# Attention and MoE in one kernel: MoE rows split where they lie and turned by DMA, bounds spread by bfloat16 products, the shift row turned in float16, buffers shared anew, a new table of times

## The chip, the cores and the metric

The kernel runs on one core of a Trainium2 chip. The metric is the device time of one execution in microseconds; the median of three runs of the kernel before is 639.03 us (638.96 to 639.34). Smaller is better. PE is the matrix engine, DVE, ACT and POOL are the vector, scalar and GpSimd engines, SP is the queue from which nearly all DMAs are issued.

## What is computed

Queries of 1152 rows are averaged in pairs to 576; 4 batches of 8 heads of softmax attention with head size 64 follow, and their result, 2304 rows of 512, goes through a layer h = x w_in, e = softmax weights of h, solu = h e, a normalisation and a product with w_out.

```python
q_pool = q.reshape(B, H, S // factor, factor, D).mean(axis=3)
scores = scale * np.matmul(q_pool, k.transpose(0, 1, 3, 2))
attn = np.exp(scores - max) ; attn = attn / (sum + 1e-09) ; attn @ v
...
h = x @ w_in
sm = e / (np.sum(e, axis=-1, keepdims=True) + 1e-09)      # e = exp(h - max)
solu = h * sm
ln = (solu - mu) / np.sqrt(var + 1e-06) * g_ln
return ln @ w_out
```

## The kernel before, in words

All factors of a product are held as two float16 parts, a high one and what it leaves (`left`, `sub`), so that a float32 product is made of three or four float16 ones. The heads run in 16 pairs P (heads g = 2P and 2P+1); the first pair works in float32. Each head has nine key blocks j, and for each block PE makes the scores, ACT their exponential twice (`expo`, float16 and float32), POOL or DVE the difference of both (`rest`), and PE the products with the values. Ahead of that stand, for each head, the row maxima (`maxima`: products, DVE reductions, then `turn`, which turns the 4 or 5 columns of maxima into rows on PE, `shift`, which scales them into float16 `c5`, and `put`, a DMA that lays them under the queries as a further row of `q2`).

For each pair there are bounds: the largest |q| (`q_turn`), a sum of |v| (`v_turn`), and for each weight matrix the largest weight (`weight_scale`). Each is a column of 128 numbers, of which every partition needs the maximum: PE turns the column, widened to 128 x 128, with a float32 product against the identity (`ident`) and DVE reduces the result. There are 16 + 15 + 2 of them. `k_hi` and `k_lo` split the keys of a pair in SBUF; `k_lo` is two DVE instructions. Keys and queries are then turned by DMA transposes on the SP queue.

The MoE part (`tokens`) has 18 tiles n of 128 rows, four for each batch and one more for every second batch. A tile is: `turn`, four float32 PE products that turn x into PSUM (line 1291 of the profile); `x_hi` (ACT) and `x_lo` (DVE), which split it out of PSUM into `xh`, `xl`; 24 products with w_in; the softmax weights (`top`, `neg`, `expo`, `weigh`), statistics (`mean`, `total`, `inverse`, `square`, five small POOL steps `factor`) and `norm`; `turn2`, eight float32 products that turn the normed rows e into PSUM (line 1379), split there by `l_hi` (ACT) and `l_lo` (DVE); 24 products with w_out; a copy and two output DMAs of 64 rows. Tiles 13 to 17 belong to the last batch and run when no attention is left (`tail`); their tiles are named `et`, `xht`, `xlt`, `lht`, `llt`.

The order of everything is set by `Plan`: each step is added with an engine, a length, the steps it needs and a due time, to which the table `OFF` adds a number for each step; a list scheduler walks all engines in time and emits the instructions of each engine in the order found. SP's queue is one of these engines, so a DMA that waits holds those behind it. `tags` says which tiles share buffers and how many there are.

Of the kernel before, what the change touches and what calls it, by code (L numbers as in the profile page):

```python
# [10 lines left out]
F32 = mybir.dt.float32  # L11
# [11 lines left out]
KP = {'W': [2, 4.44, 37.52, 4.7], 'step': 1.05, 'M': [78.33, 15.88, 7.65], 'TX': 118, 'TP': 69, 'win': 4.28, 'P': [24.74, 18.81, 12.81, 18.34, 35, 22.83], 'QP': 29, 'N': [11.98, 7], 'AV': 5.18, 'CD': [[27, 53, 2], [69, 288, 10]], 'SD': [[12, 83, 5], [70, 287, 1]], 'VM': 'BCCCBCCCBCCBCCCB', 'OF': [4.76, 1.62, 9.84, 2.47, 1.86], 'N1': 8.51, 'warm': 1, 'ws': -3.83, 'GR': 0, 'GG': 13, 'b_eh': 6, 'b_w1': 4, 'V0': -98.83, 'VF': 1, 'QD': [0, 1], 'L0': 2.74, 'F': 0, 'EX': [[10, 71, 50], [42, 282, 0]], 'LX': [3, 36.19], 'HP': [146073, 0], 'DL': 2000, 'MA': 18.0, 'TR': [2000, 2], 'P1': [-3.89, -3.14, 3.71, -7.84, -10.1, 0.03], 'WS': [47, 70, 0.22], 'KD': 5.48, 'RB': [0, 1], 'RS': [2.5, 6.5], 'LO': 0.3}  # L23
# [19 lines left out]
class Plan:  # L43
# [20 lines left out]
    def __init__(self, tags, banks, window):  # L64
        self.tags, self.banks, self.window = tags, banks, window
        self.bank = {}
        self.warm, self.warm_until = None, 0
        self.ops = []
        self.parts, self.writers, self.readers = defaultdict(dict), {}, defaultdict(list)
        self.users = defaultdict(int)  # L70

    @staticmethod
    def group(k):

        i = k[2] if k[0] in ("w32", "wm", "wi", "wo") else k[1]
        return f"{k[0]}.{i[0] if isinstance(i, tuple) else i}"

    def _keys(self, keys):
        for k in keys:
            if len(k) == 2 and self.parts[k]:  # L80
                yield from list(self.parts[k])
            yield k

    def add(self, engine, length, at, fn, reads=(), writes=(), mark=None, kind="round", also=(), calls=1, port=0):
        at += OFF.get(self.group((writes or reads)[0]), 0)
        o = Op(n=len(self.ops), engine=engine, length=length, at=at, fn=fn, mark=mark, kind=kind, calls=calls)
        o.port = port or engine == "POOL"
        deps = o.deps
# [24 lines left out]
    def run(self):  # L113
# [85 lines left out]
        while events:  # L199
            t, what, _, arg = heapq.heappop(events)  # L200
            if what == 0:
                o, done = arg, done + 1
                for b in o.uses:
                    count[b] -= 1
                    for i in where[b]:
                        last[i][o.engine] = o
                    if not count[b]:
                        for i in where[b]:
                            held[i] = None
                        for e in ready:  # L210
                            push(t, 1, e)
                for m in after[o]:
                    e = m.engine
                    hop = self.HOP[o.engine][e] + (self.LOAD[m.kind] if e == "PE" != o.engine else 0)
                    if o.engine == e and not m.deps[o]:
                        hop = 0
                    elif e == "PE" != o.engine and t > PAD[0]:
                        hop += pad
                    m.ok_at = max(m.ok_at, t + hop)
                    m.left -= 1  # L220
                    if not m.left:
                        ready[e].append(m)
                        push(m.ok_at, 1, e)
                continue
            e = arg
            if busy[e] > t:
                continue
            best = None
            limit = 1e9 if not todo else now_mark + (self.window if todo < len(marks) else FIRST)
            for o in ready[e]:  # L230
                if o.at > limit or o.ok_at > t or (best is not None and (o.at, o.n) >= (best.at, best.n)):
                    continue
                g = buffers(o)
                if g is None:
                    continue
                s = could(o, g)
                if s > t:
                    push(s, 1, e)
                    continue
                best, got = o, g  # L240
            if best is None:
                if e == "PE" and self.warm and t > KP.get("ws", 2.5) * 1000 and todo > self.warm_until:
                    i = next((i for i in range(8) if held.get(i) is None), None)
                    if i is not None:
                        extra.append((t, lambda i=i: self.warm(i)))
                        busy[e] = t + (110 if t > self.COLD else 216)
# [81 lines left out]
def attention_solu_moe(  # L328
# [17 lines left out]
    NH = B * H  # L346
    NP = NH // 2
# [1225 lines left out]
```

## Time and profile before

| | us |
|---|---|
| median of 3 runs | 639.03 |
| the profiled execution | 640.0 |
| its span, first to last instruction | 638.2 |
| PE busy | 613.8 (96%) |
| DVE busy | 514.8 (81%) |
| ACT busy | 504.8 (79%) |
| POOL busy | 451.9 (71%) |

The profiled execution is 1.0 us over the median. The granted clock of PE is 1.0 but for the stretch from 20 to 40 us, where it is 0.91. Busy time of PE counts a product from its start to its modelled end, while products overlap; so a busy PE may still have short gaps, and what a product costs in a row is read from stretches of many.

### The profile page before, as it was taken

Reading aid. Unit: us, or ns where it says so; the run is one execution under the profiler, and the core shown is the slowest. Engines: PE = TensorE matmul, PEld = TensorE weight load, DVE = VectorE, ACT = ScalarE, POOL = GpSimd, SP = SyncE. Lnnn points to the kernel's source line nnn. Section 1 sums busy time; section 2 is a strip of 40 time slices with the busy share of each in tenths; the row PEclk is TensorE's granted clock in tenths of the full one; section 3 lists DMA queues with packets and bytes.
Section 4 is the critical chain, followed back from the end, with each engine's and each line's share of the span. In section 5 each row is a group of like instructions: output and inputs, shape, how many; then the busy total and the mean of one; then the engine's idle time right before and its main releaser. Section 6 shows DMA issues by size and latency. Waiting matters only on the chain.

```text
span 638.2 us, 17474 instructions
## 1 busy us (share of the span) xinstructions
PE 613.8 (96%) x6823; PEld 398.7 (62%) x6823; DVE 514.8 (81%) x1145; ACT 504.8 (79%) x966; POOL 451.9 (71%) x485
## 2 busy tenths in 40 slices
PE   8989899999989999999999999999999999999995
PEld 8866676676555665666656655666665666564552
DVE  8998898989999889888997888989899757455451
ACT  3777797999898988899888998888897988734442
POOL 3495564576679998989988997798988798720100
PEclk9899999999999999999999999999999999999999
DMA  8476869696928673665573655755681510001102
GB/s 226 133 178 144 191 172 190 181 196 117 182 29 178 102 150 75 116 126 114 120 121 86 118 126 110 133 111 97 104 175 37 86 35 13 18 9 34 33 1 49
DMA packets 161294, 70.49 MB, mean 110 GB/s; under 512 B 150332, under 2 KB 150332, under 8 KB 161212
## 3 DMA queue, kind: packets, MB, share of 16 engines
q1 hardware_dynamic: 161212, 69.38, 52.1%
q8 instruction: 53, 0.87, 0.6%
q14 instruction: 29, 0.24, 0.1%
HBM read 36.70 MB, written 4.72 MB: 65 GB/s over the span
## 4 chain that ended last, share of the span: by engine, by line
PE 75%; DVE 12%; ACT 5%; DMA 3%; POOL 2%; issue 2%; SPq 1%; ACTq 0%; POOLq 0%; DVEq 0%
PE bank L462 68%; DVE mx L959 3%; PE bank L1379 2%; PE bank L1541 2%; POOL eh L1115 1%; DVE kn L468 1%; PE bank L1291 1%; DMA q<-c 1%; ACT eh L1094 1%; ACT e L1094 1%; DMA raw<-in_moe_w_out_dram 1%; DVE mx L954 1%; DVE x L1197 1%; ACT up L541 1%; DMA w2h<-w 1%
## 5 line engine op out<-in xcount | busy, mean ns | idle before, releaser
L1115 POOL TENSOR_TENSOR eh<-e,eh 128x512 f16<-128x512 f32 (+1 forms) x268 | 308.6, 1167 | 72.7 <-ACT e L1094 30.9
L959 DVE TENSOR_REDUCE mx<-bank 128x1 f32<-128x512 f32 (+1 forms) x300 | 186.3, 653 | 24.6 <-PE bank L462 23.8
L1094 ACT ACTIVATE eh<-bank 128x512 f16<-128x512 f32 (+3 forms) x267 | 160.7, 620 | 38.3 <-PE bank L462 37.5
L1094 ACT ACTIVATE e<-bank 128x512 f32<-128x512 f32 (+1 forms) x257 | 154.8, 617 | 14.1 <-POOL eh L1115 7.5
L462 PEld LDWEIGHTS <-eh 128*128 128x128 f16 x3112 | 130.2, 98 | 53.7 <-issue 6.4
L462 PE MATMUL bank<-vhi,eh 128*128 128x65 f16 x2070 | 139.7, 194 | 2.6 <-DVE x L1197 1.4
L462 PE MATMUL bank<-q,w 128*128 128x512 f16 (+2 forms) x576 | 139.0, 291 | 2.3 <-ACT e L1094 1.2
L462 PE MATMUL bank<-q,w2h 65*128 65x512 f16 (+1 forms) x540 | 126.5, 287 | 0.4 <-DMA q<-c 0.4
L462 PE MATMUL bank<-w,q 128*128 128x512 f16 (+2 forms) x390 | 108.3, 333 | 3.4 <-DVE mx L959 2.6
L462 PE MATMUL bank<-vlo,eh 128*128 128x64 f16 x1042 | 96.7, 193 | 0.0
L462 PEld LDWEIGHTS <-w 128*128 128x128 f16 x540 | 47.2, 99 | 22.7 <-issue 3.5
L462 PEld LDWEIGHTS <-w2h 65*128 65x128 f16 x540 | 45.2, 98 | 24.4 <-issue 3.0
L462 PE MATMUL bank<-wb,xh 128*128 128x512 f16 x208 | 60.1, 379 | 0.0
L462 PE MATMUL bank<-wb,lh 128*128 128x512 f16 x208 | 57.0, 379 | 0.0
L1362 POOL TENSOR_TENSOR st<-st 128x1 f32<-128x1 f32 x54 | 12.6, 233 | 62.3 <-ACT junk L1349 60.7
L1121 POOL TENSOR_TENSOR er<-r,er 128x320 f16<-128x320 f32 (+1 forms) x60 | 45.9, 766 | 9.3 <-ACT er L1105 3.5
L901 POOL TENSOR_TENSOR vlo<-vx,vhi 128x1152 f16<-128x1152 f32 x16 | 38.5, 2409 | 8.0 <-ACT vhi L897 8.0
L462 PEld LDWEIGHTS <-q 128*128 128x128 f16 x360 | 31.3, 99 | 19.0 <-issue 0.9
L1310 DVE TENSOR_REDUCE st<-bank 128x1 f32<-128x512 f32 x36 | 24.7, 685 | 18.4 <-PE bank L462 18.3
L468 DVE SCALAR_TENSOR_TENSOR kn<-kt,qs,kn 128x576 f16<-128x576 f32 x30 | 33.9, 1169 | 2.1 <-ACT kn L728 2.0
L679 POOL TENSOR_TENSOR qt<-qt 128x576 f32<-128x576 f32 x15 | 23.3, 1556 | 14.8 <-DMA qt<-in_q_dram 14.8
L462 PE MATMUL bank<-vx,eh 128*128 128x65 f32 x256 | 33.5, 273 | 0.2 <-DVE x L1197 0.2
(157 smaller groups left out, 1117.4 us busy)
## 6 DMA issues: line engine op xcount, KB each, us to landing
kt<-in_k_dram SPq DMA_DIRECT2D x32, 288.0 KB
qt<-in_q_dram SPq DMA_DIRECT2D x16, 576.0 KB
vx<-in_v_dram SPq DMA_DIRECT2D x32, 288.0 KB
out_dram<-o SPq DMA_DIRECT2D x36, 128.0 KB
khi<-w SPq DMA_DIRECT2D x30, 144.0 KB
w2h<-w SPq DMA_DIRECT2D x30, 144.0 KB
raw<-in_moe_w_in_dram SPq DMA_DIRECT2D x8, 511.6 KB
raw<-in_moe_w_out_dram SPq DMA_DIRECT2D x8, 511.6 KB
```

Of the source, the lines that this page charges most:

```text
L462: nc.tensor.matmul(out=o, lhsT=a, rhs=b, start=first, stop=last, skip_group_check=True)
L468: eng.scalar_tensor_tensor(out=o, in0=a, scalar=scale, in1=b, op0=ALU.mult, op1=ALU.subtract)
L679: nc.gpsimd.tensor_tensor(out=o, in0=t[:, :, 0, :], in1=t[:, :, 1, :], op=ALU.add)
L901: nc.gpsimd.tensor_tensor(out=o, in0=t, in1=h, op=ALU.subtract)
L959: nc.vector.tensor_reduce(out=tl["mx", g][:, m, c:c + 1], in_=tl["nps", (g, m, c)], op=ALU.max, axis=AXX)
L1094: nc.scalar.activation(out=o if P else o.rearrange("p (f i) -> p f i", f=2), in_=i, func=ACTF.Exp, scale=esc)
L1115: eng.tensor_tensor(out=e[:, o:o + c.stop - c.start], in0=e32[:, c], in1=e[:, c], op=ALU.subtract)
L1121: eng.tensor_tensor(out=e[:, :, 1, :], in0=tl["r32", (g, u)][:, 0:len(RU[u]), :], in1=e[:, :, 0, :], op=ALU.subtract)
L1310: nc.vector.tensor_reduce(out=st(f), in_=tl[H_[f]], op=ALU.max, axis=AXX)
L1362: nc.gpsimd.tensor_tensor(out=st(o), in0=st(a), in1=nhalf if b is None else st(b), op=op)
L1379: nc.tensor.transpose(ps[:, c, :], tl[E][:, o:o + 128], ident)
L1541: plan.warm = lambda i: nc.tensor.transpose(bank[:, i, 0:128], ident, ident)
```

## The change

**MoE rows.** x is no longer turned on PE. `x_hi` and `x_lo` split it where it lies in SBUF into the two halves of one float16 tile `xn`, and one DMA transpose on SP (`x_turn`) lays it turned into `xt`. The two steps and the DMA are due 3 units earlier than the products (`XE`). **Last tiles.** For tiles 13, 14 and 15 (`LT` 16) the normed rows go the same way: `n_hi` (ACT) and `n_lo` (DVE) split 1024 columns in SBUF, two DMA transposes turn them. Tiles 0 to 12 and 16, 17 are turned on PE as before. **Bounds.** The 33 turns are made by `spread`: the upper half of each float32 word is read as bfloat16 and multiplied by a bfloat16 identity. **Shift.** A DVE step of its own (`scaled`) makes the scaled float16 column `m6`; PE turns it in float16, and `shift` is a plain copy. **Keys.** They are loaded head by head, and `k_lo` is one instruction instead of two. **Buffers.** The float32 tiles of the first pair (`zw1`, `zq1`, `zq2`) now share four buffers with `e` and `et`; `w1` becomes a float16 tile; `lht`, `llt` share those of `q1`, `q2`; `xn`, `xt` have two each; a few tiles that were chosen by parity (`w2`, `zq`, `vhi`) follow the slot that the plan gave. **Last store.** The second output DMA of the last tile is issued by ACT. **Times.** All numbers of `OFF` are new (1015 before, 1067 now); the other constants are as before.

```diff
+    def spread(o, bound):
+        mm(o, bound.bitcast(BF16)[:, 1:2].to_broadcast([128, 128]), idb[:, 0, :], True, True)
...
-            nc.tensor.transpose(psum(("mps", P), 128), tl["qm", P][:, 0:1].to_broadcast([128, 128]), ident)
+            spread(psum(("mps", P), 128), tl["qm", P])
...
         def k_lo():
             t = tl["kn", P]
-            for h in range(2):
-                left(t[:, h, :, 1, :], tl["kt", P][:, :, h, :], tl["qs", P][:, 2:3], t[:, h, :, 0, :])
+            left(kn_part(t, 1), both(tl["kt", P]), tl["qs", P][:, 2:3], kn_part(t, 0))
...
+        def scaled():
+            nc.vector.tensor_scalar(
+                out=new(("m6", g), [128, 6], F16)[:, 0:nm], in0=tl["m5", g][:, 0:nm], scalar1=-1.0 / ONE,
+                scalar2=SHIFT * QT / ONE, op0=ALU.mult, op1=ALU.add,
+            )
+
         def turn():
-            nc.tensor.transpose(psum(("cps", g), 128, p=5)[0:nm], tl["m5", g][:, 0:nm], ident)
+            mm(psum(("cps", g), 128, p=5)[0:nm], tl["m6", g][:, 0:nm], id16, True, True)
...
-            for c in range(KI):
-                nc.tensor.transpose(ps[:, c, :], src()[:, c * 128:(c + 1) * 128], ident)
-
         def x_hi():
-            nc.scalar.activation(out=tl[XH], in_=tl[KX], func=ACTF.Copy, scale=xs[:, r, 2:3])
+            o = new(XN, [128, 2, DM], F16)[:, 0, :]
+            nc.scalar.activation(out=o, in_=src(), func=ACTF.Copy, scale=xs[:, r, 2:3])
 
         def x_lo():
-            left(tl[XL], tl[KX], xs[:, r, 2:3], tl[XH])
+            left(tl[XN][:, 1, :], src(), xs[:, r, 2:3], tl[XN][:, 0, :])
+
+        def x_turn():
+            o = new(XT, [128, 2, KI, 128], F16)
+            nc.sync.dma_start_transpose(
+                out=o.rearrange("p a c t -> p (a c) t"), in_=tl[XN].rearrange("p a d -> p (a d)")
+            )
...
+        def n_hi():
+            nc.scalar.copy(out=new(("lnh", n), [128, 2 * SQ], F16)[:, 0:DF], in_=tl[E])
+
+        def n_lo():
+            nc.vector.tensor_tensor(
+                out=new(("lnl", n), [128, 2 * SQ], F16)[:, 0:DF], in0=tl[E], in1=tl["lnh", n][:, 0:DF], op=ALU.subtract
+            )
+
+        def n_turn(k, i):
+            turned(k)
+            nc.sync.dma_start_transpose(out=tl[k], in_=tl[i, n][:, 0:DF])
...
+        if by_dma:
+            a2 = a + OF[2]
+            add("ACT", ACT(DF, 0, 1), a2, n_hi, [E], [("lnh", n)])
+            add("DVE", DVE(DF), a2, n_lo, [E, ("lnh", n)], [("lnl", n)], port=1)
+            for k, i in ((LH[0], "lnh"), (LL[0], "lnl")):
+                add("SP", TRD, a2, lambda k=k, i=i: n_turn(k, i), [(i, n)], [(*k, 0), (*k, 1)], calls=TRC)
+        for i in range(0 if by_dma else 2):
...
+                if i and n == NT_ALL - 1:
+                    add("ACT", 60, at + rate + 0.5, lambda d=d: store(*d, nc.scalar), [("o", n)], [])
```

On PE the program has 72 turns of x (64 of `x`, 8 of `xm`) and 24 of 40 turns of `et` fewer, 33 bounds and 30 shifts in 16 bit instead of float32, and 4 fewer of the idle products that keep the engine warm at the start; the number of other products is the same. After the last product with `eh` PE has 288 products of 512 columns and 68 turns before, 282 and 24 now. In its last stretch tile 17's last product with w_in stands directly ahead of tile 16's turn before; now 38 products stand between it and tile 17's own turn, and six products of tile 16 between that turn and tile 17's products. Between the last product with `eh` and the first one of tile 13 with w_in there are 12 products and then the turn of x before; now 38 products and eight turns.

The SP queue at the end of attention, before: `q` from `c` is the shift row of a head, `w2h` its keys again, `xm` the gathered rows of tile 17.

```order
L1070 DMA w2h_80<-w_9027 64x1152
L980 DMA q_9059<-c_9513 1x4x128
L982 DMA q_9059<-c_9513 1x2x64
L1445 DMA out_dram<-o 64x512 x2
L1465 DMA xm<-x 64x512
L1070 DMA w2h_81<-w_9211 64x1152
L980 DMA q_9059<-c_9844 1x4x128
L1445 DMA out_dram<-o 64x512 x2
L1465 DMA xm<-x 64x512
L1445 DMA out_dram<-o 64x512 x14
```

The same place now; `xt` from `xn` is a tile's x, `lht` and `llt` are the normed rows of a last tile.

```order
L1079 DMA w2h_81<-w_9049 64x1152
L1301 DMA_TRANSPOSE xt<-xn 128x8x128
L985 DMA q_9066<-c_9904 1x4x128
L1471 DMA out_dram<-o 64x512 x2
L1494 DMA xm<-x 64x512
L1301 DMA_TRANSPOSE xt<-xn 128x8x128 x2
L1471 DMA out_dram<-o 64x512 x2
L1301 DMA_TRANSPOSE xt<-xn 128x8x128
L1471 DMA out_dram<-o 64x512 x2
L1301 DMA_TRANSPOSE xt<-xn 128x8x128
L1402 DMA_TRANSPOSE lht<-lnh 128x8x128
L1402 DMA_TRANSPOSE llt<-lnl 128x8x128
```

A transpose of tile 12's x now stands directly ahead of the last head's shift row, and the queue of the last tiles holds eleven transposes where there were only stores.

DVE at the end of attention, before: `x` is the divided result of the last head, `xlt` the low part of a tile's x, `e` tile 12's rows.

```order
L1197 TENSOR_TENSOR x<-bank,r 128x5x64
L468 SCALAR_TENSOR_TENSOR xlt<-bank,xs,xht 128x512
L1366 TENSOR_SCALAR e<-e,st 128x1024
L1310 TENSOR_REDUCE st<-bank 128x1
L465 TENSOR_TENSOR ll<-bank,lh 128x512
```

The same place now, with `xn` in the place of `xlt`.

```order
L1206 TENSOR_TENSOR x<-bank,r 128x5x64
L1370 TENSOR_SCALAR e<-e,st 128x1024
L470 SCALAR_TENSOR_TENSOR xn<-x,xs,xn 128x512 x2
L463 TENSOR_TENSOR ll<-bank,lh 128x512 x2
L470 SCALAR_TENSOR_TENSOR xn<-x,xs,xn 128x512 x2
L1316 TENSOR_REDUCE st<-bank 128x1 x2
```

The norm of tile 12 moved ahead of the split of x, and the split of all four tiles of the last batch stands together, with two SBUF inputs (`x`, `xn`) each instead of one from PSUM and one from SBUF.

## Rows read from the trace of the kernel before

**Rows 1.** Busy time by stretch: PE, PEld, DVE, ACT, POOL (instructions), clock, DMA share.

```profile
0.00:195.00 195.00, 180.28 (x1952) 133.44 (x1953) 176.48 (x383) 158.78 (x291) 122.81 (x136) 0.99 0.73 162
195.00:560.00 365.00, 362.23 (x4490) 228.70 (x4489) 301.95 (x678) 315.54 (x618) 320.68 (x320) 1.00 0.51 101
560.00:638.20 78.20, 71.25 (x389) 36.55 (x385) 36.39 (x85) 30.50 (x60) 8.47 (x31) 1.00 0.12 26
```

**Rows 2.** Chain that ended last, by line: 0 to 195, 195 to 560, 560 to the end.

```profile
by line: PE bank L462 29.5%; DVE mx L959 9.7%; PE bank L1541 5.7%; issue 4.7%; DMA q<-c 3.5%; DVE kn L468 3.3%; DMA raw<-in_moe_w_out_dram 2.6%; POOL eh L1115 2.5%; ACT eh L1094 2.3%; ACT e L1094 2.1%; DVE mx L954 1.9%; ACT up L541 1.7%; DM
by line: PE bank L462 86.5%; PE bank L1379 2.9%; issue 1.3%; PE bank L1291 1.2%; POOL eh L1115 1.2%; DVE mx L959 0.7%; PE bank L968 0.6%; DVE kn L468 0.6%; DVE e L1366 0.5%; DVE eh L1108 0.4%; ACT eh L1094 0.4%; ACT e L1094 0.4%; POOL er L1
by line: PE bank L462 79.6%; PE bank L1379 5.8%; PE bank L1291 2.7%; ACT o L1440 1.7%; ACT lht L1385 1.5%; DVE et L1366 1.0%; issue 0.3%; ACTq L1440 0.0%
```

**Rows 3.** The same chain in order of time, from 560: start, us, what.

```profile
563.70 0.44 PE bank L1291 x4
...
572.78 0.87 PE bank L1291 x8
573.65 9.93 PE bank L462 x46
...
593.95 0.87 PE bank L1379 x8
...
625.09 0.70 ACT o L1440
...
625.80 0.82 DVE et L1366
...
626.67 0.67 PE bank L1379 x4
...
628.00 5.37 PE bank L462 x24
```

**Rows 4.** Line 1291 alone, the turns of x, in the three stretches: PE, PEld.

```profile
0.00:195.00 195.00, 1.27 (x8) 0.84 (x8) 0.99 0.73 162
195.00:560.00 365.00, 6.86 (x44) 5.37 (x44) 1.00 0.51 101
560.00:638.20 78.20, 2.83 (x20) 2.37 (x20) 1.00 0.12 26
```

**Rows 5.** Groups by form: count, busy us, mean ns of one, idle before.

```profile
L462 PE MATMUL bank<-w,q 128*128 128x128 f16 x120 | 11.6, 218 | 0.2 <-DVE mx L959 0.2
L864 PE MATMUL bank<-ident,am 128*128 128x128 f32 x16 | 4.5, 279 | 0.8 <-DVE mx L959 0.8
L968 PE MATMUL bank<-ident,m 128*5 128x128 f32 x15 | 4.1, 273 | 0.4 <-DVE m L965 0.4
L965 DVE TENSOR_REDUCE m<-mx 128x5 f32<-128x15 f32 x15 | 2.4, 160 | 0.1
```

**Rows 6.** One line on DVE, the splits: count, ns least/median/most, first and last start.

```profile
L468 DVE SCALAR_TENSOR_TENSOR kn<-kt,qs,kn x30: 796/819/2793, 30.9 to 485.7; 128x576 f16<-128x576 f32 x30
L468 DVE SCALAR_TENSOR_TENSOR qb<-qt,qs,qa x15: 796/1078/1709, 32.8 to 491.8; 128x576 f16<-128x576 f32 x15
L468 DVE SCALAR_TENSOR_TENSOR xl<-bank,xs,xh x13: 732/740/752, 163.1 to 545.9; 128x512 f16<-128x512 f32 x13
```

**Rows 7.** Timeline: start, us, engine, instruction; a key transpose, a last turn, the last stores.

```profile
490.26 1.34 SPq L738 DMA_TRANSPOSE w<-kn  x1
...
618.42 1.04 PE L1379 MATMUL bank<-ident,et 128*128 128x128 f32 x8
...
634.15 1.11 SPq L1445 DMA_DIRECT2D out_dram<-o  x2
```

**Rows 8.** Busy time of the stretch in which that key transpose moves (columns of Rows 1).

```profile
491.50:492.75 1.25, 1.25 (x36) 1.01 (x33) 1.25 (x3) 0.62 (x2) 0.77 (x1) 1.00 1.04 236
```

**Rows 9.** Waits of the SP queue, 195 to 560: us in total, times, longest us.

```profile
SPq L644 <- DVE qb L468: 25.3, 5, 10.0
...
SPq L980 <- DVE c L971: 23.0, 4, 11.5
```

More of the change, by code (lines that the diff above doesn't have):

```diff
@@ L82, in _keys, with place @@
             yield k
+    @staticmethod
+    def place(k):
+        return ("z" + k[0], *k[1:]) if k[0] in ("w1", "q1", "q2") and k[1] < (2 if k[0] == "w1" else 1) else k
     def add(self, engine, length, at, fn, reads=(), writes=(), mark=None, kind="round", also=(), calls=1, port=0):
@@ L87, in add @@
         o.port = port or engine == "POOL"
+        reads, writes, also = ([self.place(k) for k in x] for x in (reads, writes, also))
         deps = o.deps
@@ L391, in attention_solu_moe @@
     tag(1, "qa")
-    tag(5, "w1", "et", "lht", "llt")
-    tag(2, "q1", "xht")
-    tag(2, "q2", "xlt")
+    tag(KP["ZB"], "zw1", "zq1", "zq2", "e", "et")
+    tag(5, "w1")
+    tag(2, "q1", "lht")
+    tag(2, "q2", "llt")
     tag(2, "w2")
@@ L426, in new @@
     def new(key, shape, dtype):
-        t, bufs = tags[key[0]]
+        t, bufs = tags[Plan.place(key)[0]]
         tl[key] = sb.tile(shape, dtype, tag=t, name=key[0], bufs=bufs)
-        return tl[key]
-    def new16(key, p, n):
-        t = new(key, [p, 2 * n], F16)
-        tl[key] = t[:, 0:n]
         return tl[key]
@@ L582, in turn @@
         def turn():
-            nc.tensor.transpose(psum(("mps", -1 - m), 128), t[:, 0:1].to_broadcast([128, 128]), ident)
+            spread(psum(("mps", -1 - m), 128), t[:, 0:1])
         def every():
@@ L597, in weight_scale @@
         add("DVE", (1 + m) * 80, at, top, [("wm", m), *([("g", 0)] if m else [])], [("ws", m, 0)])
-        add("PE", TR(1), at, turn, [("ws", m, 0)], [("mps", -1 - m)], kind="whole")
+        add("PE", MH(128), at, turn, [("ws", m, 0)], [("mps", -1 - m)], kind="half")
         add("DVE", 340 + 140 * m, at, every, [("mps", -1 - m), ("ws", m, 0)], [("ws", m, 1)])
@@ L633, in load_k @@
         def load_k():
[L634 removed]
+            kt = new(("kt", P), [128, 2, NJ, D], F32)
             for i in range(2):
[L636 removed]
+                nc.sync.dma_start(out=kt[:, i], in_=k[b, h0 + i].rearrange("(p j) d -> p j d", j=NJ))
         def load_k0(i):
@@ L709, in pair @@
             add("DVE", DVE(SQ) + 4, a, q_top, keys, [("qm", P, 0)])
-            add("PE", 60, a, q_turn, [("qm", P)], [("mps", P)], kind="whole")
+            add("PE", MH(128), a, q_turn, [("qm", P)], [("mps", P)], kind="half")
             add("DVE", DVE(128), a, q_all, [("mps", P)], [("qs", P, 0)])
@@ L768, in prep_k @@
             add("ACT", ACT(2 * SQ, 1, 1), at, k_hi, [KT, S_], [(*KN, 0)])
-            add("DVE", 1455, at, k_lo, [KT, S_, (*KN, 0)], [(*KN, 1)], port=1)
+            add("DVE", 1326, at, k_lo, [KT, S_, (*KN, 0)], [(*KN, 1)], port=1)
             for h in range(2):
@@ L861, in v_turn @@
         def v_turn():
-            am = tl["am", P]
-            nc.tensor.transpose(psum(("vps", P), 128), am[:, 0:1].to_broadcast([128, 128]), ident)
+            spread(psum(("vps", P), 128), tl["am", P])
         def v_all():
@@ L1041, in maxima @@
         add("DVE", 83, a, reduce_all, [("mx", g)], [("m5", g)])
-        add("PE", TR(1), a, turn, [("m5", g)], [("cps", g)], kind="whole")
+        add("DVE", 72, a, scaled, [("m5", g)], [("m6", g)])
+        add("PE", MH(128), a, turn, [("m6", g)], [("cps", g)], kind="half")
         add("DVE", 200, a, shift, [("cps", g)], [("c5", g)])
@@ L1317, in expo @@
         def expo(f):
-            if f == 0 and tail:
-                tl[E] = big(E, dtype=F32)[:, 0:DF]
-            elif f == 0:
-                new(E, [128, DF], F32)
+            if f == 0:
+                tl[E] = new(E, [128, S], F32)[:, 0:DF]
             nc.scalar.activation(
@@ L1368, in norm, with turned @@
             )
+        def turned(k):
+            t = new(k, [128, 2 * SQ], F16)
+            tl[k] = t[:, 0:DF].rearrange("p (a b) -> p a b", a=KO)
         def turn2(i):
@@ L1390, in tokens @@
         step = rate / 12
-        add("PE", TR(KI), at, turn, [key], [KX], also=[XH, XL], kind="whole")
         SX = ("xs", r, 1)
-        add("ACT", ACT(512, 1), at, x_hi, [KX, SX], [XH])
-        add("DVE", DVE(512) + 68, at, x_lo, [KX, XH, SX], [XL])
+        add("ACT", ACT(512, 1, 1), at - KP["XE"], x_hi, [key, SX], [(*XN, 0)])
+        add("DVE", 660, at - KP["XE"], x_lo, [key, (*XN, 0), SX], [(*XN, 1)], port=1)
+        add("SP", TRD, at - KP["XE"], x_turn, [XN], [XT], calls=TRC)
         for f in range(2):
@@ L1418, in tokens @@
             prev(a + OF[4])
-        for i in range(2):
+        if by_dma:
[5 more added lines that the diff above has]
+        for i in range(0 if by_dma else 2):
             a2 = a + OF[2] + OF[3] * i
@@ L1442, in copy, with store @@
                 )
-            def store(p0, rows, dst):
-                nc.sync.dma_start(out=dst, in_=tl["o", n][p0:p0 + rows, :])
+            def store(p0, rows, dst, eng=nc.sync):
+                eng.dma_start(out=dst, in_=tl["o", n][p0:p0 + rows, :])
             for c in range(12):
```

95 lines of the change are left out of this document (45 added, 50 removed).

## The prediction

> **What bounds the kernel now.** I read the busy times by stretch first, then the chain of waits. From 195 to 560 us PE is busy 362.2 of 365 us while POOL, the next, has 320.7 (88%), ACT 315.5 and DVE 302.0 (83%) [rows 1]; the chain there runs over PE's lines for 91% (86.5, 2.9, 1.2 and 0.6) [rows 2]. From 560 on it is PE for 88%, and the rest is a few steps at the very end [rows 2, 3]. Before 195 the chain is a mixture: PE 29.5%, PE's idle products 5.7%, DVE's reductions 9.7%, DMAs, ACT and POOL in small shares, with DVE busy 176.5 of 195 us, about as much as PE [rows 1, 2]. So PE time taken away should come back nearly whole after 195 us, and only in part before. What a PE instruction is worth is read from stretches of many: eight turns take 0.87 us, so 0.109 each [rows 3], and 46 products of 512 columns 9.93 us, so 0.216 each [rows 3]. The means of single instructions contain their flight and are used for differences alone.
>
> **The change part by part.** The sum is made against the profiled execution, 640.0 us, which is 1.0 over the median.
>
> x turned by DMA. The 72 turns go: 8 before 195 us (0.87), 44 in the middle (4.80), 20 after 560 (2.18) [rows 3, 4]. In their place SP issues 18 transposes. The nearest row is a key transpose of 1152 columns (x has 1024): SP is held 1.34 us and the data move from 491.5 to 492.75 [rows 7, 8], so 2.5 us from issue to landing on a free queue. In the middle the split is due three units ahead of its products and 11 tiles come in 365 us, so that latency is covered by some 30 us of other work for each. At the end of attention it must be covered by PE work: before, x is turned at 563.70 [rows 3], some 12 products (2.6 us) behind the last attention product; now split (0.7 on ACT as for a copy of 512 columns, 0.74 on DVE) [rows 3, 6] and transpose (2.5) put it at 6.5 us, and 38 products and eight turns (8.2 + 0.9 = 9.1 us) stand ahead. Covered; without that cover it would cost 3.5 us once.
>
> Normed rows by DMA, tiles 13 to 15. 24 turns go, all after 560: 2.62 us [rows 3]. Split and transposes are again waited for only if other products run out; from tile 13's last product with w_in to its first with w_out stand 70 products, 15.1 us. Softmax to norm took tile 17 8.2 us in the run before (618.42, when its products were issued, to 626.67) [rows 3, 7]; two splits of 1024 columns (at most twice 0.70 and 0.74, 2.9 [rows 3, 6]) and 2.5 for the transpose make 13.6. Covered by 1.5.
>
> The last tile. Before, PE stands still from 625.07 to 626.67 for tile 17's norm, and some 0.2 twice for the casts behind turns [rows 3]. The new order puts 38 products, 8.2 us, between tile 17's last product and its turn, the same length as the 8.2 that the chain takes, and six products of another tile behind the turn. Of 2.0 us I take 1.7 as saved; the bounds are 0 and 2.0. One output DMA issued by ACT beside SP's saves half of 1.11 [rows 7]: 0.5.
>
> Bounds and shifts. A bfloat16 or float16 product of 128 columns has a mean of 218 ns, the float32 ones 279 and 273 [rows 5]: 33 x 0.061 + 30 x 0.055 = 3.7 us, spread over the attention, so 1.2 before 195 and 2.5 behind. Against that stands one more DVE step for each of 30 heads. No row shows `m6`; it is bounded by nothing and by a split's 0.74 [rows 6], 0 to 22 us. I take the reduction of the same five columns right ahead of it, 0.16 [rows 5], so 4.8 us.
>
> Other DVE work. The key split becomes 15 instructions instead of 30. 576 columns take 796 ns at least and 512 columns 732, so a column costs 1 ns and an instruction some 220 beside; each joined pair saves that, 3.3 us, and up to 2.0 where the second one waited [rows 6]. x_lo now reads two SBUF inputs. The form from PSUM never left 732 to 752 ns; splits from SBUF spread from 796 to 2793 (median 819) and 1709 (median 1078) [rows 6], so they wait for something that a PSUM form does not. Bounds for the 18: 0 and 2.0 us each; I take 0.35 (the median of the query split over its least is 0.28). Sum for DVE: 4.8 - 3.3 + 6.3 = 8 us, two thirds of it in the middle, where DVE has 63 to spare [rows 1]. Not on the path, but it can delay single reductions.
>
> The Trainium skill has a rule that speaks against this part: SBUF — State Buffer, section "Who interferes with whom", says that a DVE instruction with two SBUF inputs contends with a GpSimd instruction that reads SBUF, that the port is an exclusive lock, and that the loser waits for the whole instruction. The trace agrees in that only splits from SBUF spread. Its result is the rival "the middle does not follow", below.
>
> The sum. After 560: 2.18 + 2.62 + 1.7 + 0.5 = 7.0. Middle: 4.80 + 2.5 = 7.3, of which I take 90% by the chain's share, 6.5. Before 195: 0.87 + 1.2 = 2.1, of which a third by the chain's share, 0.7. Together 14.2: 640.0 - 14.2 = 625.8, and 1.0 less against the median: 624.8. I say **625.0**.
>
> **The rivals.**
> 1. The middle does not follow. POOL has 88% of the stretch already [rows 1]; the splits of 13 tiles (those of the last five fall where POOL is empty) can each hold it for 0.75 us and be held for up to 2.0 [rows 6], and a PE that runs 2% faster asks more of POOL. Then the PE time saved before 560 turns into waits for `eh`, and only the end's 7.0 remain: 639.0 - 7.0 = 632. For it: POOL's share. Against it: the chain in the middle passes `eh` on POOL for 1.2% [rows 2], and the joined key splits give back lock time.
> 2. The SP queue holds the shift rows. A transpose of x stands directly ahead of a head's shift row; SP waits in order, and waits of up to 10.0 and 11.5 us for a DVE step occur now [rows 9], harmless while nothing urgent is behind. If x_lo comes late by w behind other DVE work, the row `q2` and all scores of that head come late. 13 tiles in the attention: it cancels the 14.2 from w = 1.1 us of lost PE time each; with w = 1.5 it is 639.0 + 19.5 - 14.2 = 644, slower. For it: an in-order queue with 24 more waits, and a chain that runs over that row for 3.5% of the first stretch. Against it: in the middle the row is not in the chain at all [rows 2].
> 3. The new times fit better than the old. Beside PE the chain has 9% in the middle, 32 us, and two thirds of the first 195 us. If all PE time returns (2.2 more) and two more of these waits go, it is 621.
> 4. It saves nothing on balance: w near 1.1 in rival 2, or turned rows that land too late at the end, 639.
>
> **How the numbers follow.** Forecast 0.60, with a range of its own of 622 to 629 (the 2.0 of the last tile whole or none, the middle at 60% to 100%); rival 1 0.15; rival 3 0.10; rival 2 0.11; rival 4 0.04. Faster is forecast, 1 and 3: 0.85; within 0.2%, about what a measurement of this kernel can tell from no change, is 4: 0.04; slower is 2: 0.11. The range 621 to 633 holds the forecast, most of rival 1 and half of rival 3, so 8 in 10.
>
> **What would show it.** In the trace after: no line of x turns on PE, 16 turns of `et`, and no gap of 1.6 us before the last one; the stretch from the last product with `eh` to the last product shorter by 8 us, of which 1.3 are six products that moved ahead; the middle's PE gaps as small as now. Right for the DMA part if landings are 2 to 3 us behind issue and no product of `xt`, `lht` or `llt` waits for a DMA. Rival 1 shows as waits of PE for `eh` and of POOL beside long splits; rival 2 as waits of PE for `q2` rows with SP held at a transpose. The prediction is wrong if PE waits more than 5 us in all for DMA-turned rows, or if the gain lies before 195 us.

## The result, and the profile after

| | before | changed kernel |
|---|---|---|
| median, us | 640.14 (637.91 to 643.97, 18 runs) | 643.82 (639.22 to 649.07, 18 runs) |
| ratio | | 1.0055, 95% interval 1.0031 to 1.0079 |
| the profiled execution, its span | 640.0, 638.2 | 639.95, 638.0 |

The forecast was 625.0 us, faster; the changed kernel is slower by half a per cent. Its time varies more than that of before, and it goes with the granted clock of PE: runs with a mean of 0.994 to 0.995 took 639.2 to 640.3 us, the two with 0.977, which the ratio leaves out, 648.8 and 649.1. The profiled run has 0.995 and took as long as the profiled one of before: its trace shows where the forecast gain of 14 us went, and not the last 4 us of the loss.

The busy times of the page, and by stretch (columns of [rows 1]):

```profile
PE 606.9 (95%) x6718; PEld 385.1 (60%) x6723; DVE 526.0 (82%) x1157; ACT 505.3 (79%) x963; POOL 459.2 (72%) x485
```

```profile
0.00:195.00 195.00, 176.87 (x1897) 130.44 (x1903) 176.31 (x376) 154.99 (x282) 118.91 (x129) 0.98 0.70 163
195.00:560.00 365.00, 356.53 (x4359) 217.46 (x4359) 310.72 (x690) 313.18 (x614) 325.42 (x321) 1.00 0.51 110
560.00:638.00 78.00, 73.46 (x464) 37.15 (x462) 38.94 (x93) 37.12 (x69) 14.86 (x37) 1.00 0.31 63
```

Against [rows 1] PE is busy 3.4 us less before 195 and 5.7 us less in the middle, while DVE is busy 8.8 us more there. The end has more products because attention ends late. The last four products with `eh`, in the timeline of before and then of after; the fourth starts 0.09 us behind the first:

```profile
560.71 0.29 PE L462 MATMUL bank<-vhi,eh 128*128 128x65 f16 x4
```

```profile
569.50 0.29 PE L460 MATMUL bank<-vhi,eh 128*128 128x65 f16 x4
```

From the start of the fourth to the end of the span it is 77.4 us before (638.2 - 560.8) and 68.4 now (638.0 - 569.6). So the end became 9.0 us shorter and everything ahead of it 8.8 us longer, though it has fewer PE instructions. The chain of the middle shows what came in ([rows 2] has 91% on PE's lines; here 73%):

```profile
by line: PE bank L460 71.2%; DVE mx L961 6.4%; PE bank L1387 1.9%; DVE m L970 1.9%; issue 1.6%; DVE vx L895 1.5%; DVE e L1370 1.4%; POOL eh L1124 1.3%; DVE st L1316 1.2%; DMA xt<-xn 1.1%; DVE ll L463 1.0%; DVE mx L956 1.0%; DVE kn L470 1.0%
```

L970 is the new scaling step. Its groups by form, and its line alone (least, median and most ns, and who waited for it):

```profile
L970 DVE TENSOR_SCALAR m<-m 128x5 f16<-128x5 f32 x15 | 11.7, 780 | 0.3
L970 DVE TENSOR_SCALAR m<-m 128x4 f16<-128x4 f32 x15 | 8.4, 560 | 0.3
```

```profile
L970 DVE TENSOR_SCALAR m<-m x30: 149/634/1912, 54.4 to 548.9; 128x5 f16<-128x5 f32 x15, 128x4 f16<-128x4 f32 x15
...
  PEld L460: 12.0, 14
  PE bank L460: 7.7, 10
```

Four or five columns take 0.15 us at best and 0.67 on the mean, 20.1 us in all; PE waits 7.7 us for them, and its weight loads (PEld) 12.0. One of them in the timeline, with what POOL and PE do:

```profile
160.20 1.00 DVE L970 TENSOR_SCALAR m<-m 128x4 f16<-128x4 f32 x1
...
158.91 3.38 POOL L1124 TENSOR_TENSOR eh<-e,eh 128x512 f16<-128x512 f32 x3
...
160.62 0.38 PE L460 MATMUL bank<-q,w2h 65*128 65x512 f16 x1
161.26 0.22 PE L460 MATMUL bank<-id,m 128*4 128x128 f16 x1 [0.25 <-DVE m L970]
...
163.83 0.22 PE L460 MATMUL bank<-vhi,eh 128*128 128x65 f16 x1 [1.94 <-DVE qs L700]
```

POOL's three instructions are some 1.13 us each (3.38 / 3), so the second ends near 161.17; the step that began at 160.20 ends at 161.20, and PE's turn starts 0.06 behind it. It is so in the whole trace: 25 of the 30 steps take over 0.2 us, and each of the 25 ends 21 to 31 ns behind the end of a POOL instruction; of the five quick ones, three fall where POOL does nothing.

The pause of 1.94 us behind it, which ends with a column `qs` from DVE, is for the most part not the step's. The kernel without the step (the first experiment) pauses nearly as long at the same place:

```profile
159.49 0.19 PE L460 MATMUL bank<-vhi,eh 128*128 128x65 f16 x1 [1.66 <-DVE qs L700]
```

Behind the 1.94 us the changed kernel's clock is down for some microseconds, at a mean of 0.57 between its two levels (1.2 and 2.4 GHz), which costs about 4.0 x 0.43 = 1.7 us; behind the 1.66 us it stayed at 1.00.

```profile
163.50:167.50 4.00, 3.67 (x60) 3.12 (x60) 2.73 (x8) 3.94 (x9) 0.42 (x1) 0.57 1.04 219
```

A wait for the step itself can be followed by this too, and need not be. The longest early one, in the changed kernel and then in the run that keeps the step and widens the turn (below), each with the stretch behind it (columns of [rows 1]; the clock is 1.00 and 0.50):

```profile
55.20 0.22 PE L460 MATMUL bank<-id,m 128*5 128x128 f16 x1 [1.70 <-DVE m L970]
...
56.00:58.00 2.00, 2.00 (x29) 1.97 (x27) 0.69 (x1) 1.81 (x3) 0.00 (x0) 1.00 0.51 77
```

```profile
55.65 0.29 PE L460 MATMUL bank<-id,m6s 128*128 128x128 f16 x1 [1.71 <-DVE m6s L971]
...
56.00:58.00 2.00, 2.00 (x20) 1.78 (x19) 0.36 (x2) 0.96 (x2) 0.17 (x1) 0.50 0.68 101
```

So the step can cost clock beside its waits; how much it does in the changed kernel as a rule, no trace here shows.

### The profile page after: what moved, and what is told of

The parts are those of the page before. It is cut to its first block, busy times and chain, and to the rows that moved or that the text cites. A ratio compares the mean times of both kernels' runs of the same rounds, so it can differ in the third digit from the quotient of the medians.

```text
span 638.0 us, 17320 instructions
## 1 busy us (share of the span) xinstructions
PE 606.9 (95%) x6718; PEld 385.1 (60%) x6723; DVE 526.0 (82%) x1157; ACT 505.3 (79%) x963; POOL 459.2 (72%) x485
## 4 chain that ended last, share of the span: by engine, by line
PE 65%; DVE 27%; issue 3%; ACT 2%; DMA 1%; POOL 1%; SPq 0%; DVEq 0%; POOLq 0%; ACTq 0%
PE bank L460 61%; DVE mx L961 8%; DVE m L970 2%; PE bank L1570 2%; PE bank L1387 2%; DVE kn L470 1%; DVE mx L956 1%; DVE qb L470 1%; DVE vx L895 1%; DVE wb L553 1%; DVE wb L470 1%; DVE wm L559 1%; DVE e L1370 1%; DVE x L1206 1%; DVE st L1316 1%
## 5 line engine op out<-in xcount | busy, mean ns | idle before, releaser
L1124 POOL TENSOR_TENSOR eh<-e,eh 128x512 f16<-128x512 f32 (+1 forms) x268 | 312.8, 1184 | 84.1 <-ACT e L1103 23.6
L1103 ACT ACTIVATE eh<-bank 128x512 f16<-128x512 f32 (+3 forms) x267 | 159.1, 619 | 37.2 <-PE bank L460 35.8
L460 PEld LDWEIGHTS <-eh 128*128 128x128 f16 x3112 | 128.7, 98 | 56.3 <-issue 9.8
L460 PE MATMUL bank<-q,w 128*128 128x64 f16 (+2 forms) x576 | 138.6, 291 | 2.9 <-ACT eh L1103 1.6
L460 PE MATMUL bank<-wb,xt 128*128 128x512 f16 x432 | 114.0, 379 | 0.0
L460 PEld LDWEIGHTS <-xt 128*128 128x128 f16 x432 | 38.3, 98 | 35.5 <-issue 0.7
L1366 POOL TENSOR_TENSOR st<-st 128x1 f32<-128x1 f32 x54 | 15.7, 291 | 49.8 <-ACT junk L1353 38.3
L460 PEld LDWEIGHTS bank<-vx,eh 128*128 128x128 f32 x256 | 31.9, 190 | 2.5 <-DVE qs L700 0.6
```

Of the source, the lines that this page charges most:

```text
L460: nc.tensor.matmul(out=o, lhsT=a, rhs=b, start=first, stop=last, skip_group_check=True)
L1103: nc.scalar.activation(out=o if P else o.rearrange("p (f i) -> p f i", f=2), in_=i, func=ACTF.Exp, scale=esc)
L1124: eng.tensor_tensor(out=e[:, o:o + c.stop - c.start], in0=e32[:, c], in1=e[:, c], op=ALU.subtract)
L1366: nc.gpsimd.tensor_tensor(out=st(o), in0=st(a), in1=nhalf if b is None else st(b), op=op)
```

## Experiments

Theory L: the loss is the wait of the small step for POOL, with PE waiting in its queue. Theory X: the DMA-turned x and the splits from SBUF lose it. Theory T: the new table of times fits badly.

**The step taken away.** Maxima are turned in float32 and scaled behind the turn, as before; no other instruction moves.

```diff
         def scaled():
-            nc.vector.tensor_scalar(out=new(("m6", g), ...), in0=tl["m5", g][:, 0:nm], ...)
+            pass
         def turn():
-            mm(psum(("cps", g), 128, p=5)[0:nm], tl["m6", g][:, 0:nm], id16, True, True)
+            nc.tensor.transpose(psum(("cps", g), 128, p=5)[0:nm], tl["m5", g][:, 0:nm], ident)
...
```

> The changed kernel with one part undone and every other instruction in its place: no scaling step on DVE, the maxima turned in float32, scaled behind the turn as before. Theory L (the scaling step, 0.67 us in the mean instead of the 0.16 I forecast, waits for a port that POOL holds, and PE waits for it at the head of its queue; PE's gaps ahead of that turn are 11.3 us in the trace after against 2.4 before): PE gets back 8 to 10 us less 1.7 for the float32 turns, and some of the stretches at half clock go: 631 to 637, ratio to the kernel before 0.985 to 0.995, and PE's gaps ahead of the turn 2 to 3 us. Rival T (the new table of times fits the chip worse, so DVE comes late whatever that step does) and rival X (the splits of x from SBUF and the 24 DMA transposes cost it): 642 to 646, as the changed kernel.

Measured: 625.5 us (625.0 to 627.9), ratio to before 0.978 (0.975 to 0.980). Lower than L's range; X and T fall, since the table, x and the splits are still the changed kernel's. The middle and its chain:

```profile
195.00:560.00 365.00, 361.53 (x4461) 224.61 (x4459) 303.86 (x676) 316.76 (x622) 326.11 (x322) 1.00 0.51 108
```

```profile
by line: PE bank L460 85.5%; PE bank L1387 2.8%; DVE mx L961 1.9%; POOL eh L1124 1.3%; DVE vx L895 0.8%; DMA w<-kn 0.8%; DVE st L1316 0.7%; DVE kn L470 0.6%; DVE eh L1117 0.6%; PE bank L973 0.5%; ACT eh L1103 0.5%; ACT e L1103 0.5%; DVE qb 
```

PE is back at 361.5 of 365 us, and attention ends at 554.6, 6.2 us ahead of the kernel before. The two profiled executions, with and without the step, are 15.0 us apart (638.0 and 623.0). Of these 8.3 are waits of PE in the list (25.7 against 17.4 us, those for the step or the maxima 7.7 against 0.9), about 1.7 the clock at 163.5, and some 4.0 the turn's narrow weights, which come further below.

**The step alone, in the kernel before.** Scaling and float16 turn, behind the reduction, in before's order.

```diff
             nc.vector.tensor_reduce(out=m5[:, 0:nm], in_=tl["mx", g][:, 0:nm], op=ALU.max, axis=AXX)
+            nc.vector.tensor_scalar(out=m6[:, 0:nm], in0=m5[:, 0:nm], scalar1=-1.0 / ONE, ...)
...
```

> The kernel before with that one part alone: the scaling step stands behind the reduction of the maxima, PE turns in float16, every other instruction in its place. Theory L: the step takes 0.5 to 0.8 us in the mean here too, PE waits 5 to 9 us more ahead of the turns, less 1.7: 643 to 648, ratio 1.005 to 1.013. Rivals T and X: 638 to 640, ratio 0.996 to 1.0, since PE's turn is 0.055 us shorter.

Measured: 665.9 us (658.8 to 667.7), 1.037 (1.032 to 1.045). Again more than L expected; X and T have no part in this kernel. 20 of the 30 steps take over 0.2 us, and all 20 end 25 to 33 ns behind a POOL instruction. Who waited for the step:

```profile
L968 DVE TENSOR_SCALAR m<-m x30: 170/532/1714, 54.6 to 565.1; 128x5 f16<-128x5 f32 x15, 128x4 f16<-128x4 f32 x15
...
  PEld L462: 19.9, 22
  PE bank L462: 11.1, 14
```

**The step twice,** in the changed kernel.

```diff
             nc.vector.tensor_scalar(out=new(("m6", g), [128, 6], F16)[:, 0:nm], in0=tl["m5", g][:, 0:nm], ...)
+            nc.vector.tensor_scalar(out=tl["m6", g][:, 0:nm], in0=tl["m5", g][:, 0:nm], ...)
```

> The changed kernel with the scaling step made twice, one behind the other, 30 more DVE instructions of 4 or 5 columns. Theory L: the second waits as the first, 0.5 to 0.7 us each, and PE waits with it: 10 to 18 us more than the changed kernel, 652 to 662, ratio 1.02 to 1.035. Rivals T and X: a step of 0.16 us, 5 us of DVE that is mostly hidden: 644 to 647.

Measured: 666.9 us (666.2 to 667.7), 1.042 (1.039 to 1.045), more than L expected: 23 us more for 30 steps, 0.77 us each with what follows from them. Both copies are slow (149/624/1893 and 170/580/1329 ns).

**The step in another shape.** The same step, in the changed kernel, reads its source three times over as three rows and writes two or five rows: three times the elements, rows that don't match.

```diff
+            rows = 2 if nm == 4 else 5
-                out=new(("m6", g), [128, 6], F16)[:, 0:nm], in0=tl["m5", g][:, 0:nm], ...
+                out=new(("m6", g), [128, 16], F16)[:, 0:3 * nm].rearrange("p (a b) -> p a b", a=rows),
+                in0=tl["m5", g][:, 0:nm].rearrange("p (o m) -> p o m", o=1).to_broadcast([128, 3, nm]), ...
```

> The changed kernel with the same scaling step in the same place, but with its source read three times over as 3 rows and its target laid as 2 or 5 rows, 12 or 15 elements instead of 4 or 5. Theory L with the port taken by the two-port form of the instruction: the form has source and target rows that do not match, so it should not take the port, and although it writes three times as much it lasts 0.15 to 0.2 us with no spread; the time is that of the undone part less the turns, 630 to 636. If the step is slow for another reason (it waits for the reduction ahead of it, or DVE is late anyway): 0.5 us or more still, 642 to 646.

Measured: 628.2 us (627.9 to 629.0), 0.981 (0.979 to 0.984), below L's range.

```profile
L971 DVE TENSOR_SCALAR m<-m x30: 143/166/172, 53.4 to 536.8; 128x15 f16<-128x15 f32 x15, 128x12 f16<-128x12 f32 x15
...
  PEld L460: 2.8, 5
  PE bank L460: 1.1, 1
```

Three times the data in a fourth of the time, and no spread. 27 of these 30 steps overlap a POOL instruction, and none waits for its end. The step is slow by its form; 15.6 of the 18.3 us between the changed kernel and the one without the step go with it. The Trainium skill names this form: by SBUF — State Buffer, section "Who interferes with whom", a `tensor_scalar` in a two-port mode takes the ports that DVE shares with GpSimd as an exclusive lock, and by VectorE: DVE Perf Modes, section "What auto-detection actually checks", the mode needs one source and a destination in SBUF with outermost sizes both even or equal. The trace agrees: equal sizes 149 to 1912 ns, 3 against 2 or 5 never over 172.

The same shape in the kernel before with the step:

```diff
-                out=m6[:, 0:nm], in0=m5[:, 0:nm], ...
+                out=m6[:, 0:3 * nm].rearrange("p (a b) -> p a b", a=2 if nm == 4 else 5),
+                in0=m5[:, 0:nm].rearrange("p (o m) -> p o m", o=1).to_broadcast([128, 3, nm]), ...
```

> The kernel before with the scaling step and the float16 turn, as in the run that took 666 us, but with the step's source read three times over as three rows and its target as two or five rows. If the step is slow by its form (source and target of like rows, which waits while POOL works), it now takes 0.15 to 0.2 us each without a spread, and the time is near the kernel before, 637 to 643. Rival: 30 steps more on DVE between the reductions and PE's turn cost that much in this order whatever their form, 655 to 667.

Measured: 644.0 us (642.3 to 647.4), 1.006 (1.004 to 1.009), just above the range, with the step at 166/169/173 ns (least, median, most). So 22 of the 26 us of the step in that kernel are its form. But 4.0 us remain, and 2.7 in the changed kernel.

**What remains: the turn of few columns.** From the kernel without the step, the reduction writes bfloat16 and the turn is a 16-bit product; nothing is added.

```diff
-            m5 = new(("m5", g), [128, 5], F32)
+            m5 = new(("m5", g), [128, 6], BF16)
...
-            nc.tensor.transpose(psum(("cps", g), 128, p=5)[0:nm], tl["m5", g][:, 0:nm], ident)
+            mm(psum(("cps", g), 128, p=5)[0:nm], tl["m5", g][:, 0:nm], idb[:, 0, :], True, True)
```

> The kernel of the run without the scaling step (625.5 us), in which the reduction of the 4 or 5 maxima writes bfloat16 and the turn is a bfloat16 product in the place of a float32 one; no instruction is added or moved. If the sum of the prediction holds (a 16-bit product of 128 columns costs 55 ns less than a float32 one, and PE time comes back nearly whole), 30 x 0.055 = 1.65 us: 623 to 625. Rival: the turn's length lies beside waits of PE and the time stays, 625 to 626.5.

Measured: 628.2 us (627.8 to 632.6), 0.983 (0.980 to 0.986): 2.7 us over the run with float32 turns by the medians, against both expectations, though the intervals of the two ratios just touch. The same place in the timelines of PE, with float32 and with bfloat16:

```profile
257.89 0.38 PE L460 MATMUL bank<-q,w2h 65*128 65x512 f16 x1
258.11 0.27 PE L973 MATMUL bank<-ident,m 128*4 128x128 f32 x1
258.22 0.19 PE L460 MATMUL bank<-vhi,eh 128*128 128x65 f16 x1
...
257.89 0.09 PEld L973 LDWEIGHTS bank<-ident,m 128*4 128x4 f32 x1
```

```profile
258.70 0.38 PE L460 MATMUL bank<-q,w2h 65*128 65x512 f16 x1
259.01 0.22 PE L460 MATMUL bank<-idb,m 128*4 128x128 bf16 x1
259.16 0.20 PE L460 MATMUL bank<-vhi,eh 128*128 128x65 f16 x1
...
259.00 0.08 PEld L460 LDWEIGHTS <-m 128*4 128x4 bf16 x1 [0.42 <-DVE vs L880]
```

The float32 weights load at 257.89, beside the product ahead; turn and next product follow at 0.22 and 0.11. The bfloat16 ones load only at 259.00: 0.31 to the turn and 0.15 to the next. So the 16-bit turn takes 0.094 + 0.150 = 0.244 us of PE where the float32 one takes 0.109; the medians over the 30 heads are 94 and 150 ns too, and 30 x 0.135 = 4.0 us. To tell width from type, the maxima were put into a zeroed tile of 128 columns, of which the turn takes 128, or different numbers:

```diff
-            m5 = new(("m5", g), [128, 6], BF16)
+            m5 = m5s[plan.slot["m5", g]]
...
-            mm(psum(("cps", g), 128, p=5)[0:nm], tl["m5", g][:, 0:nm], idb[:, 0, :], True, True)
+            w = 128
+            mm(psum(("cps", g), 128)[0:w], m5s[plan.slot["m5", g]][:, 0:w], idb[:, 0, :], True, True)
```

> The kernel of the bfloat16 maxima (628.2 us), whose turn began 94 ns late and held the next product back to 150 ns in nearly every head, where the float32 turn did neither. Here the maxima lie in the first columns of a tile of 128, the others zero, and the turn has all 128 columns as weights. If the few weight columns in 16 bit make the delay, it goes: 30 x 0.19 = 5.7 us less than the narrow one, or 30 x 0.055 = 1.65 less than the float32 one, 622.5 to 624.5. Rival: the delay belongs to bfloat16 maxima or to their coming from DVE late, whatever the width: 627.5 to 629.

> As the run with 128 columns, but the turns of different pairs have 8, 16, 32, 64, 96 or 128 columns as weights, five heads of each, to read from the trace at which width the turn is delayed by 94 ns and the next product by another 94. If few columns make it, the narrow ones show the delay and those of 128 don't; where between them it ends is open. Rival: none or all show it. Its time lies between the two others, 623 to 628.

The run of different widths took 629.5 us once; it has four turns with 8 columns, six each with 16, 32 and 64, four each with 96 and 128. Its timeline at turns of 8, 64, 96 and 128 weight columns:

```profile
429.90 0.38 PE L460 MATMUL bank<-q,w2h 65*128 65x512 f16 x1
430.21 0.22 PE L460 MATMUL bank<-idb,m5s 128*8 128x128 bf16 x1
430.36 0.20 PE L460 MATMUL bank<-vhi,eh 128*128 128x65 f16 x1
...
538.82 0.38 PE L460 MATMUL bank<-q,w2h 65*128 65x512 f16 x1
539.13 0.24 PE L460 MATMUL bank<-idb,m5s 128*64 128x128 bf16 x1
539.30 0.24 PE L460 MATMUL bank<-vhi,eh 128*128 128x65 f16 x2
...
344.64 0.22 PE L460 MATMUL bank<-idb,m5s 128*96 128x128 bf16 x1
344.69 0.38 PE L460 MATMUL bank<-wb,xt 128*128 128x512 f16 x1
...
379.65 0.38 PE L460 MATMUL bank<-q,w2h 65*128 65x512 f16 x1
379.87 0.22 PE L460 MATMUL bank<-idb,m5s 128*128 128x128 bf16 x1
379.93 0.19 PE L460 MATMUL bank<-vhi,eh 128*128 128x65 f16 x1
```

With 8 columns 0.31 and 0.15 us, with 64 0.31 and 0.17; with 96 the next product follows after 0.05, with 128 after 0.22 and 0.06. All 22 turns of up to 64 columns show both delays; of the 8 wider ones two begin 53 and 80 ns late, and the next product follows all of them within 71 ns. So in 16 bit it is the width. With 128 columns throughout the median turn begins 3 ns late instead of 94, but the time is 626.9 us (623.8 to 628.7), 0.979 (0.976 to 0.983): its interval overlaps with that of the narrow turns and with that of the float32 ones, so the expected 1.65 us under the latter didn't appear, and what the delay is worth there isn't settled by this pair.

In the changed kernel, with its step as it is:

```diff
-                out=new(("m6", g), [128, 6], F16)[:, 0:nm], in0=tl["m5", g][:, 0:nm], ...
+                out=m6s[plan.slot["m6", g]][:, 0:nm], in0=tl["m5", g][:, 0:nm], ...
...
-            mm(psum(("cps", g), 128, p=5)[0:nm], tl["m6", g][:, 0:nm], id16, True, True)
+            mm(psum(("cps", g), 128), m6s[plan.slot["m6", g]], id16, True, True)
```

> The changed kernel (643.8 us), its scaling step and its form kept, but the step writes into a zeroed tile of 128 columns and the float16 turn has all 128 as weights. If the width of the weights is a cause of its own beside the step's wait, 30 x 0.19 = 5.7 us go and the step's wait stays: 634.5 to 639. Rival: the step's wait is all of the loss, and the turn's delay lies beside it: 641 to 645.

Measured: 640.1 us (637.6 to 642.7), 0.9998 (0.997 to 1.002), against 1.0055 for the changed kernel: 3.6 us, less than the 5.7 expected, more than the rival's nothing. The two intervals lie apart. The step keeps its spread there (153/630/1901 ns), so its target tile is not what makes it slow. Width and step are two causes, and the step's form is the larger.

**Other terms of the sum,** each undone in the kernel without the step. Bounds in float32 again:

```diff
-        mm(o, bound.bitcast(BF16)[:, 1:2].to_broadcast([128, 128]), idb[:, 0, :], True, True)
+        nc.tensor.transpose(o, bound[:, 0:1].to_broadcast([128, 128]), ident)
```

> The kernel of the run without the scaling step (625.5 us), with the 33 bounds turned by float32 products again. If the prediction's term holds (33 x 0.061 = 2.0 us, nearly all of it on PE's way), 627 to 628.5. Rival: these turns lie beside waits and the change of the bounds gave nothing, 625 to 626.

Measured: 626.6 us (625.7 to 627.0), 0.978 (0.976 to 0.980), against 0.978 (0.975 to 0.980): 1.1 us by the medians and 0.2 by the ratios, neither clear of noise.

The normed rows of tiles 13 to 15 turned on PE again, by a constant:

```diff
-'LT': 16
+'LT': 13
```

> The kernel of the run without the scaling step (625.5 us), with the normed rows of tiles 13 to 15 turned on PE again, by the same table of times. If the prediction's term holds, 24 turns of 0.109 us come back on PE: 2.6 us, 627.5 to 629, and up to 630 if the order of the last tiles also opens the gaps before the last turn again. Rival: the transposes saved nothing, since waits stood in the place of the turns, 625 to 626.

Measured: 633.3 us (633.0 to 633.7), 0.989 (0.987 to 0.991): 7.8 us more, three times the turns. PE's waits from 560 on, where the kernel with DMA turns has none, and the stretch around the longest (columns of [rows 1]):

```profile
PE bank L460 <- DVE et L1333: 2.8, 1, 2.8
PE bank L1387 <- DVE et L1370: 0.3, 1, 0.3
```

```profile
597.00:601.50 4.50, 1.78 (x9) 0.69 (x7) 1.71 (x4) 2.33 (x6) 0.00 (x0) 1.00 0.25 56
601.50:606.00 4.50, 4.43 (x14) 1.65 (x14) 2.75 (x14) 3.88 (x8) 1.14 (x5) 0.63 0.01 2
```

2.6 for the turns, 2.8 for a wait that opens when an order made for DMA turns has to carry the turns on PE, and 4.5 x 0.37 = 1.7 of clock behind that wait make 7.1. The last part is an estimate that the times don't confirm: the four executions have mean clocks of 0.990 and 0.995, and those with 0.995 took 633.0 and 633.3 us, those with 0.990 took 633.2 and 633.7.

The key split in two instructions again, in the kernel with 128 weight columns:

```diff
-            left(kn_part(t, 1), both(tl["kt", P]), tl["qs", P][:, 2:3], kn_part(t, 0))
+            for h in range(2):
+                c = slice(h * NJ, (h + 1) * NJ)
+                left(kn_part(t, 1)[:, c], both(tl["kt", P])[:, c], tl["qs", P][:, 2:3], kn_part(t, 0)[:, c])
```

> The kernel with 128 weight columns, with the key split of a pair in two instructions again as before the change. It tells what the joined split is worth: the trace has 15 x 1570 ns where 30 took 33.9 us, 10.4 us of DVE time. If DVE is off the path there, as the prediction said, the time stays within 1 us of the other run; if single reductions that wait behind a split reach PE, 2 to 6 us more.

Measured: 626.8 us (626.1 to 628.9), 0.980 (0.977 to 0.983), against 626.9. Joined and in two, by group:

```profile
L470 DVE SCALAR_TENSOR_TENSOR kn<-kt,qs,kn 128x1152 f16<-128x1152 f32 x15 | 23.7, 1582 | 1.4 <-ACT kn L734 1.3
```

```profile
L470 DVE SCALAR_TENSOR_TENSOR kn<-kt,qs,kn 128x576 f16<-128x576 f32 x30 | 26.6, 927 | 1.4 <-ACT kn L734 1.3
```

2.9 us of DVE time, none of it in the result.

The best kernel seen is the first: the change without its scaling step and with the float32 turn of the maxima, 625.5 us, 2.2% under before.

## Why the prediction was wrong

**The scaling step: the step that failed.** "No row shows `m6` ... I take the reduction of the same five columns right ahead of it, 0.16" was mis-sized: it took 0.67 us on the mean and up to 1.91, where the bound for one was 0.74. The 20.1 us of all 30 lie within the 0 to 22 that the prediction gave, but the sum went on with 4.8, and neither the range nor a rival carried the rest. The reduction was near in size and place, but not in form: a reduction (140 to 174 ns in every run) does not wait for POOL, this form does. The 0.16 was a price without a wait, though the prediction saw in [rows 6] that splits from SBUF wait for something. "Not on the path" failed as well: PE's turn needs the step, and PE takes its queue in order, so every product behind the turn waits, whatever share of the stretch DVE has to spare. In the middle PE was idle for 8.5 of 365 us, where the prediction looked for gaps as small as before (2.8). Without the wait the time falls by 15.6 us.

**The float16 turn of the shift** was put down as 0.055 us saved, from a row with 128 weight columns [rows 5]. With 4 or 5 columns it costs 0.135 more. The term has the wrong sign: wide weights give back 3.6 us in the changed kernel, clear of noise. The other runs agree less clearly: 2.7 us lost with bfloat16 maxima, and 2.7 and 4.0 with the quick step, where that step is part of the loss.

**Rival 1** named the mechanism, a lock held by POOL, but put it on the two-input splits and priced the loss at the middle's gain alone, 632. The splits of x did little:

```profile
L470 DVE SCALAR_TENSOR_TENSOR xn<-x,xs,xn x16: 740/752/1545, 166.2 to 578.5; 128x512 f16<-128x512 f32 x16
L470 DVE SCALAR_TENSOR_TENSOR kn<-kt,qs,kn x15: 1401/1419/2244, 31.2 to 498.8; 128x1152 f16<-128x1152 f32 x15
```

Their mean of 908 ns (16 of them) is 0.17 over the least, where 0.35 was taken. The key splits took 10.4 us less of DVE than before (33.9 to 23.5); in one and the same order joining them saves 2.9, near the 3.3 taken; what the rest of the 10.4 came with no run shows. DVE as a whole grew by 11.2 us (514.8 to 526.0), against 8 forecast, but for another reason than given.

**What was right.** With the step gone the time is 625.5, so the sum of the rest holds to a microsecond, but by luck, with errors that cancel: the bounds gave 0 to 1.1 instead of 2.0 and the shift turn there is float32, without its 1.65, so the other terms gave 2 to 3 us more than forecast, of which the end has 0.7 (9.0 less the six moved products' 1.3, against 7.0); no run takes the rest apart. x by DMA: transposes of 1.23 to 1.65 us on SP, no wait of PE put down to one, though the chain of the middle passes `xt` for 1.1%. One that stands alone, issued at 584.07, moves its data from 585.25 to some 586.6, so 2.5 us from issue to landing, as forecast. Rival 2 did not come about. The end is 9.0 us shorter, 8 forecast, and after 560 PE waits for nothing; that the run without the DMA turns lost 7.8 rather than 2.6 + 1.7 was not seen, since the wait that opens in this order was in no term. The second store on ACT: from the end of the last product to that of the span 4.5 instead of 4.85 us, where 0.5 was taken as saved. The low end of the forecast's own range, 622, doesn't follow from the terms named for it: the last tile whole and the middle at 100% give 623.7.

```profile
L1301 SPq DMA_TRANSPOSE xt<-xn x18: 1232/1260/1647, 167.2 to 597.6; - x18
```

## What to carry to other kernels

A tiny new step between two engines is priced by its form and by who waits behind it, not by its columns: look for a row of the same operation, operand places and shape, and where there is none, let the range hold the longest wait that any instruction of the neighbour engine can cause, times the number of steps. If such a step must stand there while POOL works, give source and target unlike shapes, or scale in the copy out of PSUM (273 ns for `shift` with the scaling, 272 without). And a 16-bit turn took less of PE than a float32 one only when its weights were wide (0.057 to the next product with 128 columns, 0.109 in float32, 0.244 with 4 or 5 columns).

## What the runs showed of the hardware that was not expected

- A `TENSOR_SCALAR` of 4 or 5 columns from SBUF to SBUF took 149 to 1912 ns beside POOL, and each of the 25 that took over 0.2 us ended 21 to 31 ns behind a POOL instruction; of 12 or 15 columns in unlike rows it took 143 to 172.
- A 16-bit product with up to 64 weight columns starts 94 ns late and holds the next one to 150 to 176 ns; with 96 or 128 columns, or with 4 or 5 in float32, it does neither in most turns. Why is open.
- Pauses of PE of 1.7 to 2.8 us were followed by some microseconds at the lower clock level in some executions (1.71 in the run with wide weights, 1.94 in the changed kernel, 2.79 with tiles 13 to 15 on PE) and not in others (1.70 in the changed kernel, 1.66 without the step). What decides it is open.
